# Waits for a new q tile moved to the O products, and a shorter hand-planned tail, in a gated attention and token-mixing kernel

## The chip, the cores and the metric

The kernel runs on one core of a Trainium2 chip. The time is that of the device for one execution, in microseconds (us). Work is done by TensorE (PE; its weight loads are listed apart as PEld), VectorE (DVE), ScalarE (ACT) and GpSimd (POOL); SyncE (SP) issues nearly all DMAs, in the order of its queue. Each engine works through its own queue in order and waits on semaphores.

## The reference, cut to what matters

```python
x = A_x                                        # (1, 2048, 640)
g = sigmoid((x * gate_w).sum(-1, keepdims=True))
q, k, v = x @ wq, x @ wk, x @ wv               # 32 heads of 20 for q, one shared head for k and v
a = (softmax(q k^T * 20**-0.5) v) @ wo         # per head, heads side by side: (1, 2048, 640)
h = layernorm(x)
b = (w2^T gelu(w1^T h + b1) + b2)              # mixes the 2048 tokens, inner size 1728
return g * a + (1 - g) * b
```

## The kernel before, in words

The kernel first normalizes x and projects q, k and v, and writes q to DRAM (`q_scr`). Then attention and the token-mixing products run side by side on TensorE, in one order that a planner in the program works out when it is built.

**Attention** goes by 32 units of work, n = 0 to 31: a block of 512 queries times a group of four heads. A q tile holds one such n; it is loaded from `q_scr` by six DMAs (`load_q`, L127 to L157), and its loads are issued one to several steps before its first use. Rounding of fp32 in TensorE is met by splitting numbers in a high and a low part; the products of such parts stand side by side in the contraction, 60 or 62 rows of it. For each n there are

- 64 **max tiles** (`ms_next`, L506): a product of 128 queries with 512 keys, reduced by DVE to row maxima (L514). When all 64 are through, `ms_done` and `store_max` put the negated maxima in DRAM (`m_scr`, L542) and `fetch_max` (L549) reads them back into two rows of the q tile, so that the score product subtracts them itself;
- 16 **visits** (blocks of 128 keys), each with four score products (`qk`, L688) of 62 rows, each followed by an exponential on ACT (L700), and four **O products** (`pv_mm`, L721), which stand in four column strips of TensorE and sum p times v;
- at the end, division by the row sums and a store of the split result to DRAM (`o_scr`). In the loop this is `norm_steps`, eight small steps that are taken one after the other, one in each loop step (`settle`).

Score and max products use half of TensorE's 128 rows, 0 to 63 or 64 to 127. The planner therefore keeps two **lanes**, one per half; a product of one lane can run beside one of the other.

**The other products**, also 64 rows high, fill the lanes: b1 (w1 with h), b2 (w2 with the gelu; L836), and at the end the O projection with wo (`a_jobs`, L961), which reads the stored O of one block of 128 tokens and adds the stored b part.

**The loop** (`for j in range(n_st)`) has 244 steps: 72 with b1, 128 with b2, 44 with the O projection. A step lays eight score products, some max tiles (`wants[j]`), and its share of the other products on the lanes (`arrange`), and ends with one **burst**: the 16 O products of the two visits before (`burst`), their copy out by ACT (L742) and the addition by POOL (L743). Which max tiles stand in a step follows from `wants`, and what cannot be given yet is owed. Between steps, the queues get what is due there: loads of a new q tile every eight steps, settling steps, stores, the loads for the tail (`tail_load` at steps 221 and 241 to 243), and at step 241 the last four heads' rows of wo (`last_wo`).

**Behind the loop** stand the last 24 visits, as 12 **stretches** of two visits (`stretch`): eight score products, the last 16 max tiles in the first three stretches, and the O projection of the last five token blocks as far as their heads are done, cut into jobs (`tail_job`, L910). There are nine jobs: one whole block, four blocks up to column 384, and the same four from column 384 to 560; the sums of each are taken out by DVE (L922). The order within a stretch is the best of 400 random ones by the planner's own clock (`best_order`, `trial`). Here O is summed in one bank without copies (`visits`), and the unit before the last is finished by `turned_steps`. Last come 18 products held back for the end (`held`, L1424), 128 or 48 rows high, run while DVE finishes the last unit (L812 to L817), then the products with the last four heads' wo (`final`, L1402), their way out of the accumulators (`evict`: DVE at L1411, or ACT at L1414 with POOL at L1415), and eight stores (L1437).

Waits between engines are set by hand: `touch` names for each of these instructions which others it waits for, and declares all else independent; waits on DMAs are added by the framework where a tile is used.

Of the kernel before, what the change touches and what calls it, by code (L numbers as in the profile page):

```python
# [18 lines left out]
P = 128  # L19
# [12 lines left out]
TAIL = 24  # L32
# [7 lines left out]
def mix_kernel(ctx: ExitStack, tc: tile.TileContext, A_x, A_wq, A_wk, A_wv, A_wo,  # L40
# [91 lines left out]
    def load_q(n):  # L132
# [12 lines left out]
        def part(b, j, src):  # L145
            o = 64 * b + DH * j
            rows = q_scr[src, g * 4 * DH:(g + 1) * 4 * DH, cols]
            nc.sync.dma_start(out=f32(t[o:o + DH]), in_=rows.rearrange("(a b d) q -> b d a q", a=2, b=2)[b])
# [9 lines left out]
    qtiles = {}  # L158
# [305 lines left out]
    def touch(ins, reads=(), writes=()):  # L464
        need = []
# [251 lines left out]

    def pv_mm(u, o, first, last, i):
        for hh in range(4):
# [3 lines left out]
            touch(mm, [("p", j)], [("x", i)])  # L723
# [143 lines left out]
    whole = []  # L867
    tail = [[], []]
    loaded = []
    CUT = 3 * P  # L870
# [5 lines left out]
    def room(i):  # L876
        t, at = (u0, 3 * D * i) if i < 4 else (slot[0], 3 * D * (i - 4))
        return (t[:, at:at + 2 * D].rearrange("p (j c q) -> p j c q", j=2, q=P), f32(t[:, at + 2 * D:at + 3 * D]))

    def tail_load(i):  # L880
        if i < len(jobs):
            st, r0, r1 = jobs[i]
            cols = slice(st * P, (st + 1) * P)
            oT, yt = room(i)
            c0, c1 = r0 // P, r1 // P
            for j in range(2):
                nc.sync.dma_start(out=f32(oT[:, j, c0:c1]),
                                  in_=o_scr[j, r0:c1 * P, cols].rearrange("(c p) s -> p c s", p=P))
                if r1 > c1 * P:
                    nc.sync.dma_start(out=f32(oT[:r1 - c1 * P, j, c1]), in_=o_scr[j, c1 * P:r1, cols])  # L890
            if r0 == 0:
                nc.sync.dma_start(out=yt, in_=y_scr[cols, :])
            loaded.append(i)

    def tail_job(n):
        st, r0, r1 = jobs[n]
        oT, yt = room(n)
        acc, at, ready = {}, {}, []

        def mm(c, k, d, h, first, last):  # L900
# [7 lines left out]
            r = slice(64 * h, min(r1 - c * P, 64 * h + 64))  # L908
            region = [("x", at[d, h])]
            touch(nc.tensor.matmul(acc[d, h][:, :HD2], o[r, c, :], w[r, c, d * HD2:(d + 1) * HD2],  # L910
                                   start=first, stop=last), writes=region)
            if last:
# [5 lines left out]
                if st not in parts:  # L918
                    parts[st] = fin.tile([P, D], F32, name="yo") if r1 == D else spare_row(st)
                add = parts[st] if d in ready or r0 else yt  # L920
# [3 lines left out]
                if len(ready) == 4:  # L924
                    if r1 - r0 == D:
                        whole.append(lambda: nc.sync.dma_start(out=y_out[st * P:(st + 1) * P, :], in_=parts[st]))

        for h in range(2):
            ck = [(c, k) for c in range(r0 // P, DC) if r1 - c * P > 64 * h for k in range(3)]
            for d in range(2):  # L930
                if r0 and (st, d) in held:
                    continue
                for i, (c, k) in enumerate(ck):
                    step = lambda a=(c, k, d, h, i == 0, i == len(ck) - 1): mm(*a)
                    tail[h].append((n, ("a" if i == 0 else "e" if i == len(ck) - 1 else "f", step)))
# [104 lines left out]
    aj = [a_jobs(st) for st in range(NS - 5)]  # L1040
# [23 lines left out]
    for i, j in enumerate((221, 241, 242, 243, 243)):  # L1064
        ph[j][1].append(lambda i=i: tail_load(i))
# [131 lines left out]
    for i, (st, r0, _) in enumerate(jobs):  # L1197
        tail_job(i)
# [18 lines left out]
    left, n = 64 * NU - 16 - sum(given) - sum(wants[:at]), n_st - at  # L1217
    wants[at:] = sorted(left * (i + 1) // n - left * i // n for i in range(n))
    assert sum(given) + sum(wants[:n_st - 8]) >= 64 * (NU - 1)
    owed = 0  # L1220
    for j in range(n_st):
# [6 lines left out]
        to = owed + wants[j]  # L1228
        own = round((min(to, 9) + F_US / X_US * len(fs) - len(ss)) / 2)
        if h:  # L1230
            own = (given[0] - given[1] + to + 1) // 2
        own = min(to, max(0, own))
        before = sum(given)
        ms = [[f for f in (ms_next(x) for _ in range(c)) if f] for x, c in ((h, own), (1 - h, to - own))]
        owed = to - (sum(given) - before)
# [26 lines left out]
        if j == n_st - 3:  # L1262
            raw = last_wo()
        if j == n_st - 1:
            w_last = split_last(raw)
# [3 lines left out]
    assert sum(given) == 64 * NU - 16 and not follow  # L1269
# [18 lines left out]
    def trial(kinds, prefer):  # L1288
        line, new, banks_at, held_at = list(lane), list(fresh), list(free), dict(busy)
        dve, act, now, out = clock["dve"], clock["act"], state["at"], []  # L1290
        left = [list(x) for x in kinds]
        while any(left):
            options = []
            for k in range(4):
                if left[k]:
                    at = max(line[k % 2] + W_US * new[k % 2], now)
                    if left[k][0] in "sma":
# [161 lines left out]
```

## Time and profile before

| | |
|---|---|
| median of 3 runs | 1618.53 us (1618.27 to 1618.7) |
| the profiled execution, time | 1618.5 us |
| the profiled execution, span | 1616.5 us |
| granted TensorE clock | 0.999 |
| PE, PEld, DVE, ACT, POOL busy | 1608.8, 1123.3, 1383.9, 1261.1, 841.1 us |
| loop steps with the O projection | 1331.9 to 1539.0 us from the span's start |
| stretches | 1539.0 to 1601.2 us |
| the end | 1601.2 to 1616.5 us |

Times in the profile are microseconds from the span's start unless marked ns. A row of a timeline has start, duration, engine, line, operation, out<-in by tile names, shapes and count; the bracket at its end is idle time of the engine and what ended it. "issue" there means that nothing shown was waited for. The chain of work is followed back from the last instruction, each piece to what released it. PE's matmul ends are modelled, so PE counts as busy also where the lanes are not both full.

### The profile page before, as it was taken

The numbers are of one execution on the slowest core, as the hardware profiler recorded it, in microseconds if no ns is written. First come the engines' busy times: TensorE is split into PE (matmuls) and PEld (weight loads), VectorE is DVE, ScalarE is ACT, GpSimd is POOL, SyncE is SP. The second block draws the span as 40 slices with busy tenths as digits, with TensorE's granted clock in tenths as the row PEclk, the third lists the DMA queues.
The fourth block names the chain that finished last, engine by engine and source line by source line (L and its number), as shares of the span: only waits on it lengthen the run. The fifth ranks groups of instructions, "written<-read, shape, count | busy, mean of one in ns | idle before, by whom it ended". The sixth has DMA issues, their size and how long they took to land.

```text
span 1616.5 us, 39520 instructions
## 1 busy us (share of the span) xinstructions
PE 1608.8 (100%) x14868; PEld 1123.3 (69%) x14868; DVE 1383.9 (86%) x2629; ACT 1261.1 (78%) x2350; POOL 841.1 (52%) x927
## 2 busy tenths in 40 slices
PE   9999999999999999999999999999999999999998
PEld 7899876776776776666666666666666666666665
DVE  6689899999999999888888888888888886567754
ACT  4545677777777778878888788887888879999976
POOL 6567766777787776554554334444444433333321
PEclk9999999999999999999999999999999999999999
DMA  7665322232222232222212121112221113333221
GB/s 215 206 168 144 87 66 73 61 77 69 69 70 74 53 76 63 74 68 69 69 47 64 35 61 54 58 54 60 61 60 47 54 37 112 103 115 98 85 83 59
DMA packets 180308, 129.27 MB, mean 80 GB/s; under 512 B 41585, under 2 KB 150030, under 8 KB 180118
## 3 DMA queue, kind: packets, MB, share of 16 engines
q1 hardware_dynamic: 179830, 126.43, 27.7%
q8 instruction: 117, 1.92, 0.5%
q14 instruction: 73, 0.60, 0.1%
q10 hardware_dynamic: 288, 0.33, 0.1%
HBM read 93.57 MB, written 32.15 MB: 78 GB/s over the span
## 4 chain that ended last, share of the span: by engine, by line
PE 98%; POOL 0%; DVE 0%; DMA 0%; issue 0%; ACT 0%; POOLq 0%; SPq 0%; DVEq 0%
PE xs L721 29%; PE xs L688 18%; PE xs L506 18%; PE g L836 11%; PE g L1008 7%; PE pp L302 4%; PE pu L633 4%; PE g L961 3%; PE xs L910 1%; PE x L506 1%; PE pt L294 0%; PE pp L366 0%; PE xs L1424 0%; PE pp L191 0%; PE g L688 0%
## 5 line engine op out<-in xcount | busy, mean ns | idle before, releaser
L514 DVE TENSOR_REDUCE mp<-xs 128x1 f32<-128x512 f32 x1943 | 1196.9, 684 | 154.7 <-PE xs L688 78.4
L700 ACT ACTIVATE p<-xs 128x512 f32<-128x512 f32 (+1 forms) x1834 | 1011.7, 680 | 10.9 <-PE xs L688 6.4
L743 POOL TENSOR_TENSOR osum<-osum,part 128x512 f32<-128x512 f32 x212 | 274.2, 1294 | 604.8 <-ACT part L742 597.9
L721 PE MATMUL xs<-p,v_sb 128*32 128x512 f32 x4096 | 492.3, 598 | 0.0
L688 PE MATMUL xs<-q,kst 62*128 62x512 f32 x1339 | 476.2, 417 | 1.3 <-ACT p L700 1.3
L506 PE MATMUL xs<-kst,q 60*128 60x512 f32 x1242 | 437.4, 416 | 0.0
L688 PEld LDWEIGHTS xs<-q,kst 62*128 62x128 f32 x1339 | 235.9, 185 | 74.6 <-DVE mp L514 52.3
L742 ACT ACTIVATE part<-xs 128x512 f32<-128x512 f32 x212 | 126.8, 598 | 199.6 <-PE xs L721 197.3
L1008 PE MATMUL g<-slot,w 64*128 64x320 f32 x1728 | 266.8, 306 | 0.0
L721 PEld LDWEIGHTS xs<-p,v_sb 128*32 128x32 f32 x4096 | 106.9, 109 | 225.5 <-issue 161.0
L506 PEld LDWEIGHTS xs<-kst,q 60*128 60x128 f32 x1242 | 209.6, 184 | 73.4 <-DVE mp L514 44.4
L1008 PEld LDWEIGHTS g<-slot,w 64*128 64x128 f32 x1728 | 259.1, 184 | 1.9
L127 POOL TENSOR_TENSOR w<-wr,w 128x512 fp32r<-128x512 f32 (+1 forms) x180 | 225.5, 1255 | 34.5 <-ACT w L124 22.1
L688 PE MATMUL xs<-slot,kst 62*128 62x512 f32 x567 | 206.9, 418 | 0.4 <-DVE row L922 0.2
L506 PE MATMUL xs<-kst,slot 60*128 60x512 f32 x573 | 205.3, 418 | 0.0
L836 PE MATMUL g<-u,w 64*128 64x320 f32 x1296 | 201.7, 306 | 0.0
L836 PE MATMUL g<-slot,w 64*128 64x320 f32 x1296 | 201.5, 306 | 0.0
L836 PEld LDWEIGHTS g<-u,w 64*128 64x128 f32 x1296 | 195.6, 184 | 1.7
L836 PEld LDWEIGHTS g<-slot,w 64*128 64x128 f32 x1296 | 195.6, 184 | 1.5
L688 PEld LDWEIGHTS xs<-slot,kst 62*128 62x128 f32 x567 | 99.7, 185 | 31.7 <-DVE mp L514 22.6
L506 PEld LDWEIGHTS xs<-kst,slot 60*128 60x128 f32 x573 | 96.2, 184 | 33.1 <-DVE mp L514 20.4
L961 PE MATMUL g<-slot 64*128 64x320 f32 x660 | 106.7, 306 | 0.0
(197 smaller groups left out, 1483.7 us busy)
## 6 DMA issues: line engine op xcount, KB each, us to landing
wr<-in_B_w_dram SPq DMA_DIRECT2D x155, 256.0 KB
q<-q_scr SPq DMA_DIRECT2D x126, 80.0 KB
rb<-r_scr SPq DMA_DIRECT2D x120, 64.0 KB
slot<-o_scr SPq DMA_DIRECT2D x22, 320.0 KB
y_scr<-yo SPq DMA_DIRECT2D x16, 320.0 KB
q_scr<-qh SPq DMA_DIRECT2D x19, 256.0 KB
q_scr<-ql SPq DMA_DIRECT2D x19, 256.0 KB
o_scr<-rb SPq DMA_DIRECT2D x120, 40.0 KB
```

Of the source, the lines that this page charges most:

```text
L127: nc.gpsimd.tensor_sub(wl, wr, f32(wh))
L302: nc.tensor.matmul(pp, w, t, start=first and n == 0, stop=not more and n == len(steps) - 1)
L506: mm = nc.tensor.matmul(ms, qtiles[n][64 * b:64 * b + 60, pr, qt * P:(qt + 1) * P], kst[64 * b:64 * b + 60, kq * NB:(kq + 1) * NB], start= ...
L514: red = nc.vector.tensor_reduce(out, ms, axis=AX.X, op=ALU.max)
L688: mm = nc.tensor.matmul(s, kst[64 * b:64 * b + 62, kb * P:(kb + 1) * P], q[64 * b:64 * b + 62, pr, :], start=True, stop=True)
L700: act = nc.scalar.activation(p_all[:, a * NB:(j + 1) * NB], s, AF.Exp, scale=SCALE)
L721: mm = nc.tensor.matmul(o[32 * hh:32 * hh + 32, :], v_sb[:, units[u][1], :], p_all[:, j * NB:(j + 1) * NB], start=first, stop=last, skip_g ...
L742: touch(nc.scalar.activation(part, o, AF.Copy), [("x", i)])
L743: nc.gpsimd.tensor_add(osum[n], osum[n], part)
L836: other_tile(half, nc.tensor.matmul(hold["p"][:, :HD2], w[r, fc % HS, :], u[d][r, fc, :], start=(hold["n"] == 1), stop=(hold["n"] == 6 * F ...
L961: other_tile(half, nc.tensor.matmul(hold["p"][:, :HD2], o[r, c, :], w[r, c, d * HD2:(d + 1) * HD2], start=(hold["n"] == 1), stop=(hold["n" ...
L1008: other_tile(half, nc.tensor.matmul(hold["p"][:, :HD2], w[r, st % HS, :], h[d][r, st, :], start=(hold["n"] == 1), stop=(hold["n"] == 6 * NS)))
```

## The change

It has five parts.

1. A burst's first O products each also wait for one of the six DMAs that load the q tile whose max tiles come first in the next step (`arrived`, `q_loads`; `touch` gets the list `also`). `share` is the rule that splits a step's max tiles over the lanes, taken out of the loop so that the burst can ask for the next step.
2. TAIL is 16 instead of 24: 248 loop steps and 8 stretches. A twelfth token block goes through `a_jobs` in the loop.
3. All max tiles stand in the loop, spread over the O-projection steps without the last three; the last maxima are stored one step sooner behind their split, and `fetch_max` for the last unit is called from the visit where every other unit's is.
4. The tail's jobs are four: blocks 14 and 15 up to column 384, blocks 12 and 13 up to 560, each summed in one go. So that the last 48 rows of blocks 12 and 13 can lie on different lanes, `move_wo` copies the rows of wo that they need to partitions 64 and up, and block 13's O is loaded there. `last_wo` moves to the loop's second last step, `split_last` to the first stretch; three settling steps are taken per stretch. The order search takes 300 random orders and then 3000 small mutations of the best.
5. All four pairs (block, half) of blocks 14 and 15 are held for the end, 24 products instead of 18, in the order of the column block, not of the pair: first all twelve of 48 rows, then all twelve of 128. At the end DVE empties six of the eight accumulators instead of five.

```diff
-TAIL = 24
+TAIL = 16
@@ part (load_q)
+            ins = nc.sync.dma_start(out=f32(t[o:o + DH]), in_=rows.rearrange("(a b d) q -> b d a q", a=2, b=2)[b])
+            q_loads.setdefault(n, []).append(ins)
@@ pv_mm
-            touch(mm, [("p", j)], [("x", i)])
+            touch(mm, [("p", j)], [("x", i)], [arrived.pop(0)] if arrived else [])
@@ tail
-    jobs = [(NS - 5, 0, D)]
-    jobs += [(st, 0, CUT) for st in range(NS - 4, NS)] + [(st, CUT, HEAD) for st in range(NS - 4, NS)]
-    held = ((NS - 2, 0), (NS - 2, 1), (NS - 1, 0))
+    jobs = [(st, CUT) for st in (NS - 2, NS - 1)] + [(st, HEAD) for st in (NS - 4, NS - 3)]
+    held = tuple((st, d) for st in (NS - 2, NS - 1) for d in range(2))
...
+    def move_wo():
+        for i, w in enumerate((wo_hi, wo_lo)):
+            t = slot[0][:, i * D:(i + 1) * D]
+            nc.sync.dma_start(out=f32(t[64:64 + HEAD - (DC - 1) * P]), in_=f32(w[:HEAD - (DC - 1) * P, DC - 1, :]))
+            low_wo.append(t)
@@ loads of the tail
-    for i, j in enumerate((221, 241, 242, 243, 243)):
-        ph[j][1].append(lambda i=i: tail_load(i))
+    for j, (st, _) in zip((241, 242, 243, 244), jobs):
+        ph[j][1].append(lambda st=st: tail_load(st, 0, CUT))
+    ph[n_st - 8][1].append(move_wo)
@@ burst
+        if len(wants) > us[1] // 2 + 2:
+            counts = share(us[1] // 2 + 2)
+            n = max((given[b] + counts[b] - 1) // 32 for b in range(2))
+            if n in qtiles:
+                arrived.extend(q_loads.pop(n, ()))
@@ fetch_at
-        if kb == 11 and n + 2 < NU:
+        if kb == 11 and n + 1 < NU:
@@ max tiles
-    left, n = 64 * NU - 16 - sum(given) - sum(wants[:at]), n_st - at
-    wants[at:] = sorted(left * (i + 1) // n - left * i // n for i in range(n))
+    left, n = 64 * NU - sum(given) - sum(wants[:at]), n_st - 3 - at
+    wants[at:] = sorted(left * (i + 1) // n - left * i // n for i in range(n)) + [0] * 3
@@ loop, between steps
+            if len(row_max) == NU and follow:
+                follow.pop(0)()
+                stores.pop()()
...
-        if j == n_st - 3:
+        if j == n_st - 2:
             raw = last_wo()
@@ best_order
-        for _ in range(400):
+        for _ in range(300):
...
+        for n in range(3000):
+            order = list(best[1])
+            for _ in range(rng.choice((1, 1, 2, 3))):
+                order.insert(rng.randrange(len(order)), order.pop(rng.randrange(len(order))))
+            score = trial(kinds, order)
+            if score[0] <= best[0]:
+                best = score
@@ stretch
-            ms = [("m", ms_next(b)) for _ in range((3, 3, 2)[i] if i < 3 else 0)]
...
-        settle()
-        settle()
-        pop_chain()
-        if i in (7, 8):
-            tail_load(2 * i - 9)
-            tail_load(2 * i - 8)
+        if i == 0:
+            w_last.extend(split_last(raw))
+        for _ in range(3):
+            settle()
+        if i in (2, 3):
+            for st in range(NS + 2 * i - 8, NS + 2 * i - 6):
+                tail_load(st, CUT, HEAD)
@@ held products
-    for st, d in held:
-        oT, _ = room(jobs.index((st, CUT, HEAD)))
-        for c in range(DC - 1, CUT // P - 1, -1):
-            r = min(P, HEAD - c * P)
+    for c in range(DC - 1, CUT // P - 1, -1):
+        r = min(P, HEAD - c * P)
+        for st, d in held:
+            oT, _ = room(st)
@@ end
-                evict(i, d, (i, d) in ((1, 0), (1, 1), (2, 1), (3, 1)))
+                evict(i, d, (i, d) not in ((0, 1), (2, 0)))
```

More of the change, by code (lines that the diff above doesn't have):

```diff
@@ L918, in mm @@
                 if st not in parts:
[L919 to L920 removed]
+                    parts[st] = spare_row(st)
+                add = parts[st] if d in ready else yt
                 ready.append(d)
@@ L1195, in burst @@
         fresh[:] = [True, True]
-    for i, (st, r0, _) in enumerate(jobs):
+    for i in range(len(jobs)):
         tail_job(i)
@@ L1227, in mix_kernel @@
         fs, rest, done = ph[j]
[L1228 to L1235, printed above, removed]
+        counts, before = share(j), sum(given)
+        ms = [[f for f in (ms_next(x) for _ in range(counts[x])) if f] for x in (h, 1 - h)]
+        owed = sum(counts) - (sum(given) - before)
         pop_chain()
@@ L1376, in next_acc @@
         return i
-    assert not tail[0] and not tail[1] and not any(later) and not whole
+    assert not tail[0] and not tail[1] and not any(later)
     pool = pools["last"]
```

124 lines of the change are left out of this document (57 added, 67 removed).

## The prediction

> **What bounds the kernel now.** I read the shares of the page's chain first, then a table of windows cut at the starts of O-product bursts, then the end of the timeline.
>
> ```profile
> PE 98%; POOL 0%; DVE 0%; DMA 0%; issue 0%; ACT 0%; POOLq 0%; SPq 0%; DVEq 0%
> ```
>
> TensorE carries 98% of the chain, so the change is worth what it takes off TensorE's own queue. The windows below are, in order: the 26 loop steps with four max tiles, the 18 with five, the first four stretches behind the loop, the other eight, and the end. The first columns are length, PE, PEld, DVE, ACT and POOL busy; PE is busy all the time up to the last eight.
>
> ```profile
> 1331.90:1452.08 120.18, 120.18 (x1120) 75.00 (x1119) 74.29 (x152) 116.80 (x234) 40.69 (x39) 1.00 0.36 109
> 1452.08:1538.98 86.90, 86.90 (x794) 54.20 (x793) 60.70 (x121) 81.49 (x163) 27.51 (x27) 1.00 0.33 98
> 1538.98:1561.59 22.61, 22.61 (x197) 14.44 (x197) 14.56 (x29) 17.06 (x35) 6.66 (x8) 1.00 0.27 85
> 1561.59:1601.15 39.56, 39.19 (x359) 24.50 (x358) 15.07 (x30) 32.28 (x66) 1.90 (x2) 1.00 0.16 44
> 1601.15:1616.50 15.35, 10.98 (x75) 7.11 (x74) 6.61 (x16) 4.01 (x9) 2.61 (x3) 0.93 0.24 86
> ```
>
> So an O-projection step costs 120.18/26 = 4.62 us with four max tiles and 86.90/18 = 4.83 us with five; the first four stretches average 5.65 us, the last eight 4.945 us. ScalarE is busy 116.80/26 = 4.49 us of each four-tile step (nine instructions: eight exponentials, one copy of the O sum) but only 32.28/8 = 4.04 us of a late stretch, which has no copy. From 1331.90 to 1601.15 there are 56 such pieces in 269.25 us; after the change there are 56 as well, 48 steps and 8 stretches.
>
> **Part 1: O products take over the waits for a new q tile.** In the b2 stage a step runs from one burst to the next. A plain step and one with the first max products of a new tile:
>
> ```profile
> 1247.44 1.92 PE L721 MATMUL xs<-p,v_sb 128*32 128x512 f32 x16
> 1253.01 1.92 PE L721 MATMUL xs<-p,v_sb 128*32 128x512 f32 x16
> 1258.69 0.64 PE L721 MATMUL xs<-p,v_sb 128*32 128x512 f32 x4
> ...
> 1297.90 1.92 PE L721 MATMUL xs<-p,v_sb 128*32 128x512 f32 x16
> 1303.59 0.64 PE L721 MATMUL xs<-p,v_sb 128*32 128x512 f32 x4
> L506 PEldq EVENT_SEMAPHORE  x64: 51/51/51, 626.1 to 1303.1; - x64
> ...
> 1603.75 0.13 PEld L721 LDWEIGHTS xs<-p,v_sb 128*32 128x32 f32 x4 [0.30 <-issue]
> ```
>
> Plain: 5.57 us. New tile: 5.68 and, at the end of the stage, 5.69 us. The row of L506 counts the separate wait instructions ahead of max products in this stage: 64, four for each of 16 tiles, 51 ns each and always already satisfied. They stand between row-tiled products, where the queue has no slack: 0.11 us a tile, 16 x 0.11 = 1.8 us. In the earlier b1 stage a step has more max tiles and the excess is unclear; I count nothing. In the O-projection stage ScalarE is busy 97% and I also count nothing.
>
> What it adds: six waits on the first six O products of one burst per tile. The burst's weight loads run ahead of the products and then idle 0.30 us in every group of four (last row, from a late burst), and all but the first carry no wait now. The first already waits for ScalarE, so it may need one separate 51 ns wait, which can run while the last max products finish. I take 0; the ends are 0 and 0.11 us a tile (the whole price again), and more only where a load is late, which is rival (c). Whoever is behind these products on TensorE waits with them, so the loads must have landed:
>
> ```profile
> 1241.54 2.19 SPq L148 DMA_DIRECT2D q<-q_scr  x6
> ```
>
> This tile's first max products are in the step that begins at 1253.01 us; its six loads are all issued by 1243.73 us, so the burst comes 9.3 us later. Part 1: -1.8 us (0 to -2.1, the latter with three tiles of b1).
>
> **Part 2: four more steps, eight stretches, no max tiles behind the loop.** Before, 194 max tiles fall on 44 steps (26 with 4, 18 with 5) and 16 on three stretches. After, 210 fall on 45 steps: 15 with 4, 30 with 5; the last three steps have none. Those three exist nowhere now. From below, ScalarE still does its nine instructions, 4.49 us; from above, a four-tile step, 4.62 us. I take 4.50, since four max products fewer leave TensorE shorter than that; if ScalarE overlaps better, 4.3 is possible.
>
> For the stretches, two rows of the chain, with the bursts that begin and end one of them:
>
> ```profile
> 1581.81 1.85 PE xs L721 x16
> ...
> 1586.62 1.85 PE xs L721 x16
> ```
>
> The eight stretches have 180 row-tiled projection products (90 a lane) where the last eight had some 165 (88 and 77): lanes even at last, the longer one 2 products longer. A fifth max tile, 512 columns wide, adds 0.21 us to a step; a projection product has 320 columns, 0.13 us by its width: +0.3 us by the longer lane, and +1.0 us if the 15 products in all share two lanes without any slack. Each of the four jobs now sums all its columns in one go, so DVE empties 16 accumulators in 8 stretches instead of 30 in 12. The order search also tries 3000 mutations instead of only 400 random orders. The best stretch now took 1586.62 - 1581.81 = 4.81 us against 4.945 on average, so some 0.13 a stretch is there; I take 0.05, -0.4 in all.
>
> The last max rows must reach the q tile before the first stretch.
>
> ```profile
> 1528.54 0.62 POOL L982 MEMSET yo<- 128x640 f32 x1
> 1549.35 1.30 POOL L770 TENSOR_TENSOR osum<-osum,rb 128x512 f32<-128x512 f32 x1 [6.35 <-DMA rb<-r_scr]
> ...
> 1531.73 1.48 SPq L985 DMA_DIRECT2D yo<-in_A_wo_dram  x4
> 1545.16 2.55 SPq L767 DMA_DIRECT2D rb<-r_scr  x4
> 1560.87 2.75 SPq L549 DMA_DIRECT2D slot<-m_scr  x4
> ...
> 1561.60 1.95 DMA slot<-m_scr
> ...
> 1566.92 1.90 PE xs L721 x16
> ...
> PE xs L688 <- DMA slot<-m_scr: 0.2, 1, 0.2
> ```
>
> Now this path costs 0.2 us of waiting. After, count from the burst of step 245 (zero). The store of the maxima waits for DVE's work behind that step's products, 0.5 by estimate; then SP's four rb loads behind it, landed 4.2 us later as here (1545.16 to 1549.35) at about 5; POOL's scaling 1.3 and the memset of the last wo rows 0.6, to 7; SP's four wo loads 1.5, to 8.5; only then the four m loads, 0.69 us apart, landing 1.95 us after issue at 10.4, 11.1, 11.8 and 12.5. The first stretch begins two steps and a burst later, 4.5 + 4.5 + 1.9 = 10.9. The lane that needs the last two loads may stop for up to 1.6 us, depending on where its first score product stands; I take 0.6. The present 0.2 us goes, with the stretch in which it stands (1561.59 to 1566.92, 5.3 us against 4.945 on average): -0.4.
>
> The other loads I count as covered. Those of columns 384 to 560 follow the turned O tile of unit 30; a third settling per stretch brings that chain forward by about a stretch, and they are needed from the end of the fourth stretch on. If they are late, that stretch and the next wait, which the bound below takes in.
>
> Sum: 15 x 4.62 + 30 x 4.83 + 3 x 4.50 = 227.7; stretches 39.56 + 0.3 - 0.4 + 0.6 - 0.4 = 39.7; together 267.4 against 269.25: -1.9 us. Ends: steps at 4.3 (-0.6), every stretch at 4.81 (38.5 instead of 39.1 without the stall, -0.6) and no stall (-0.6) give -3.7; steps at 4.62 (+0.4), products by their sum (+0.7), a 1.6 us stall (+1.0) and no better order (+0.4) give +0.7. The two copies of wo rows and one more row block's loads are issued on SP some steps ahead of the chain of the m rows, which waits for other engines at its start; were SP full there, each would push it by 0.37 us (1.48/4).
>
> **Part 3: the end.** Weight loads, products, and what follows them:
>
> ```profile
> 1604.72 0.44 PEld L1424 LDWEIGHTS xs<-slot,slot 48*128 48x128 f32 x3 [0.84 <-issue]
> 1605.35 0.45 PEld L1424 LDWEIGHTS xs<-slot,slot 128*128 128x128 f32 x3 [0.19 <-issue]
> ...
> 1604.72 3.89 PE L1424 MATMUL xs<-slot,slot 48*128 48x320 f32 x18
> 1607.13 0.42 DVE L817 TENSOR_TENSOR q<-part,q 128x256 fp32r<-128x256 f32 x1
> 1608.45 1.04 PE L1402 MATMUL xs<-row,q 128*128 128x320 f32 x6
> 1611.45 1.74 POOL L1415 TENSOR_TENSOR p<-p,row 128x320 f32<-128x320 f32 x2 [0.38 <-ACT p L1414]
> 1612.17 0.55 DVE L1411 SCALAR_TENSOR_TENSOR p<-xs,g_col,row 128x320 f32<-128x320 f32 x1 [0.33 <-PE xs L1402]
> 1613.22 0.90 ACTq L1437 DMA_DIRECT2D out_dram<-p  x2
> ```
>
> The held products end when the final ones begin, and what these need from DVE is there at 1607.55, so held products are on the path. The 18 come in six groups of three, alternately 48 and 128 rows. The second group starts 0.63 us after the first, of which the three loads take 0.44 and the idle time at the change of height 0.19. After: 24 products as twelve of 48 rows, then twelve of 128: 24 x 0.15 + 2 x 0.19 = 3.98 us against 3.89: +0.1 us, where 24 at the present mean would be +1.3. The Trainium skill ("TensorEngine Tiling (Array Packing)", Key Properties) says that changing the tiling mode drains TensorE while changing tiles within a mode does not; that agrees with the idle 0.19 us ahead of each group here.
>
> Then the last two stores wait on ScalarE's queue for POOL's add of row block 3, left half, done at 1613.19, while DVE is done with the right half at 1612.72. DVE takes that half over: its last operation starts at 1612.17; with one more of 0.55 us just ahead of it, it ends about 0.2 us later, so the last store is issued about 0.6 us earlier. Part 3: -0.5 us (-0.8 to +0.8).
>
> Sum: -1.8 - 1.9 - 0.5 = -4.2 us. The profiled execution took 1618.5 us (span 1616.5), the median of the runs is 1618.53, so both give 1614.3 us.
>
> **The rivals.** (a) The waits only move, or the separate wait instructions stay: part 1 is nothing, 1616.1 us. For it: the first O product has its wait slot taken. Against: 0.30 us of slack in each group of loads.
> (b) The stretches give the gain back: fuller lanes (+1.0 instead of +0.3), a 1.6 us stall and no better order make part 2 +0.3, 1616.5 us. For it: the SP order above. With (a) as well 1618.3.
> (c) Slower: a burst now stands until the last of six loads has landed. Place: the burst ahead of a tile's first use, 28 tiles; it decides from (4.2 + 3.2)/28 = 0.26 us a tile; 0.5 us of stop would give 1614.3 + 14 = 1628 us. Against: 9.3 us between issue and burst here, and loads land within 2 to 4.2 us in the rows above. The rule that speaks for it: the Trainium skill ("DMA: Bandwidth & Descriptors", Rules for kernel authors) advises to wait on a DMA's semaphore late, and this change waits earlier; no row here shows a q load landing that late.
>
> **How the numbers follow.** A measurement of this kernel tells about 0.2%, 3.2 us, from no change, so faster means under 1615.3. The forecast, 1612 to 1615.3 on its own, gets 0.64; (a) 0.12 and (b) 0.14 fall within 0.2%; (c) and other late data on SP's queue 0.10. Faster 0.64, same 0.26, slower 0.10. The range from 1611.8 (the better ends of all three parts, -2.1 - 3.7 - 0.8) to 1617.0 (past (a) or (b) alone, short of both) leaves 2 in 10 out.
>
> **What would show it.** Right: new-tile steps of the b2 stage at 5.57 us and the 64 separate waits gone; 30 steps of 4.83, three near 4.5; stretches near 4.95 with the first one longer; held products in about 4.0 us with two height changes; last store on ScalarE's queue before POOL matters. Wrong: bursts longer than 1.92 us with a DMA as releaser, a wait of score products for m rows over 1.6 us, or stretches over 5.1 us.

## The result

The changed kernel took 1613.24 us (median of 7 runs, 1612.93 to 1613.6), the kernel before beside it 1618.35 us (7 runs, 1618.06 to 1618.94): a ratio of 0.9967, 95% interval 0.9959 to 0.9976. That is 5.1 us faster (3.9 to 6.6 by the interval), against 4.2 forecast. The profiled execution took 1613.6 us, its span 1611.7 us against 1616.5.

In the page of the changed kernel, the busy times and the shares of the chain of waits:

```profile
PE 1603.9 (100%) x14865; PEld 1118.7 (69%) x14865; DVE 1378.1 (86%) x2622; ACT 1262.4 (78%) x2353; POOL 844.7 (52%) x930
...
PE 99%; ACT 1%; POOL 0%; DVE 0%; issue 0%; DVEq 0%; POOLq 0%
```

TensorE is still the chain; the gain is 4.9 us of its busy time (1608.8 before). The stages are cut at the same places as in the prediction, at starts of O-product bursts. First the b2 stage, from the burst of step 71 to that of step 198, of the kernel before and then of the changed one; columns are length, then PE, PEld, DVE, ACT and POOL busy, granted clock, DMA share and GB/s.

```profile
618.69:1331.90 713.21, 713.21 (x6638) 480.04 (x6636) 637.68 (x1191) 581.23 (x1049) 325.59 (x353) 1.00 0.20 58
```
```profile
618.83:1329.92 711.09, 711.09 (x6638) 477.07 (x6637) 637.76 (x1193) 581.31 (x1049) 325.35 (x353) 1.00 0.20 58
```

Then the rest of the changed kernel: 15 steps with four max tiles, 30 with five, the three without any, the first stretch, the second, the other six, and the end:

```profile
1329.92:1399.31 69.39, 69.39 (x646) 43.24 (x646) 43.54 (x89) 67.11 (x135) 21.41 (x21) 1.00 0.37 110
1399.31:1544.23 144.92, 144.92 (x1322) 90.33 (x1321) 101.43 (x203) 135.66 (x271) 46.73 (x44) 1.00 0.36 106
1544.23:1556.96 12.73, 12.73 (x118) 7.84 (x117) 1.73 (x8) 12.43 (x27) 6.19 (x8) 1.00 0.21 56
1556.96:1562.78 5.82, 5.51 (x49) 3.53 (x48) 1.65 (x4) 5.55 (x12) 4.53 (x6) 1.00 0.35 112
1562.78:1567.84 5.06, 5.06 (x49) 3.20 (x48) 2.83 (x6) 4.44 (x10) 1.00 (x1) 1.00 0.12 28
1567.84:1596.10 28.26, 28.26 (x277) 17.72 (x276) 6.77 (x13) 23.71 (x48) 1.90 (x2) 1.00 0.15 38
1596.10:1611.70 15.60, 11.07 (x82) 7.98 (x80) 7.51 (x18) 3.76 (x8) 1.74 (x2) 0.99 0.24 86
```

| | before, us | after, us | difference | forecast |
|---|---|---|---|---|
| b2 stage | 713.21 | 711.09 | -2.12 | -1.8 |
| ahead of it | 618.69 | 618.83 | +0.14 | 0 |
| 48 steps and 8 stretches (before: 44 and 12) | 269.25 | 266.18 | -3.07 | -1.9 |
| the end, from the last burst | 15.33 | 15.63 | +0.30 | -0.5 |

The sum is -4.75 us; the spans differ by 4.8. (The ends of the last row are unrounded; the window rows cut at the span's rounded end.) Two terms were larger than forecast, and the end came out with the wrong sign.

The waits in the b2 stage: two plain bursts and one ahead of a new tile's first max products, and the separate wait instructions at the O products in that stage.

```profile
1245.66 1.92 PE L724 MATMUL xs<-p,v_sb 128*32 128x512 f32 x16
1251.24 1.92 PE L724 MATMUL xs<-p,v_sb 128*32 128x512 f32 x16
1256.80 0.64 PE L724 MATMUL xs<-p,v_sb 128*32 128x512 f32 x4
```
```profile
L724 PEldq EVENT_SEMAPHORE  x16: 51/51/51, 623.9 to 1295.5; - x16
```

The 64 separate waits at the max products are gone. One per tile has come up at the O products, 51 ns, but the step with the new tile (1251.24 to 1256.80) takes 5.56 us, like the plain one (5.58).

The first stretch waits for max rows. SP's and POOL's queues ahead of it, and the separate waits on TensorE's queue ahead of the score products of the first stretch (1557 to 1563 us):

```profile
1549.81 1.77 SPq L770 DMA_DIRECT2D rb<-r_scr  x4
1555.30 1.41 SPq L989 DMA_DIRECT2D yo<-in_A_wo_dram  x4
1556.76 2.80 SPq L550 DMA_DIRECT2D slot<-m_scr  x4
```
```profile
1553.42 1.28 POOL L773 TENSOR_TENSOR osum<-osum,rb 128x512 f32<-128x512 f32 x1 [0.77 <-DMA rb<-r_scr]
1554.64 0.63 POOL L986 MEMSET yo<- 128x640 f32 x1
```
```profile
L689 PEldq EVENT_SEMAPHORE  x2: 51/51/51, 1559.6 to 1560.9; - x2
```

This is the queue that the prediction laid out: rb loads, POOL's scaling and memset, the wo loads, and only then the four m loads. Counted from the burst of step 245 (1548.47 us), they have landed 10.4, 11.1, 11.7 and 12.4 us later; the prediction had 10.4, 11.1, 11.8 and 12.5. The two waits end 0.08 us behind the landing of the second and of the fourth load (1559.55 and 1560.87 us), and the score products with these rows start at once behind them. The profile's list of waits puts this pause down to ScalarE (`PE xs L689 <- ACT p L701`); the landings show that it is the m rows.

The held products' weight loads, which show the heights (first figure of "48*128" is the rows):

```profile
1599.67 0.45 PEld L1436 LDWEIGHTS xs<-slot,u 48*128 48x128 f32 x3 [0.84 <-issue]
...
1601.62 0.45 PEld L1436 LDWEIGHTS xs<-slot,u 128*128 128x128 f32 x3 [0.19 <-issue]
...
1603.35 0.77 PEld L1414 LDWEIGHTS xs<-row,q 128*128 128x128 f32 x5
```

24 products with one change of height inside. From the first load (1599.67) to the first load of the final products behind them it is about 3.7 us, against 3.6 (1604.72 to 1608.31) for 18 before.

### The profile page after: what moved, and what is told of

It reads as the page before. It is cut to its first block, busy times and chain, and to the rows that moved or that the text cites. A ratio compares the mean times of both kernels' runs of the same rounds, so it can differ in the third digit from the quotient of the medians.

```text
span 1611.7 us, 39437 instructions
## 1 busy us (share of the span) xinstructions
PE 1603.9 (100%) x14865; PEld 1118.7 (69%) x14865; DVE 1378.1 (86%) x2622; ACT 1262.4 (78%) x2353; POOL 844.7 (52%) x930
## 4 chain that ended last, share of the span: by engine, by line
PE 99%; ACT 1%; POOL 0%; DVE 0%; issue 0%; DVEq 0%; POOLq 0%
PE xs L724 30%; PE xs L689 18%; PE xs L507 18%; PE g L839 11%; PE g L1012 7%; PE pp L303 4%; PE pu L634 4%; PE g L965 3%; PE x L507 1%; PE xs L919 1%; PE pp L367 0%; ACT p L701 0%; PE pt L295 0%; PE xs L1436 0%; PE pp L192 0%; PE g L919 0%
## 5 line engine op out<-in xcount | busy, mean ns | idle before, releaser
L701 ACT ACTIVATE p<-xs 128x512 f32<-128x512 f32 (+1 forms) x1840 | 1013.9, 678 | 4.0 <-PE xs L689 2.9
L746 POOL TENSOR_TENSOR osum<-osum,part 128x512 f32<-128x512 f32 x216 | 279.2, 1293 | 615.5 <-ACT part L745 599.1
L689 PE MATMUL xs<-q,kst 62*128 62x512 f32 x1344 | 477.0, 418 | 1.3 <-ACT p L701 1.3
L507 PE MATMUL xs<-kst,q 60*128 60x512 f32 x1242 | 432.8, 415 | 0.0
L689 PEld LDWEIGHTS xs<-q,kst 62*128 62x128 f32 x1344 | 236.6, 185 | 74.8 <-DVE mp L515 53.9
L689 PE MATMUL xs<-slot,kst 62*128 62x512 f32 x568 | 206.2, 417 | 0.3 <-ACT p L701 0.3
L689 PEld LDWEIGHTS xs<-slot,kst 62*128 62x128 f32 x568 | 99.6, 185 | 30.5 <-DVE mp L515 21.8
L965 PE MATMUL g<-slot 64*128 64x320 f32 x720 | 118.2, 306 | 0.0
```

The costliest lines, as they stand in the source:

```text
L507: mm = nc.tensor.matmul(ms, qtiles[n][64 * b:64 * b + 60, pr, qt * P:(qt + 1) * P], kst[64 * b:64 * b + 60, kq * NB:(kq + 1) * NB], start= ...
L689: mm = nc.tensor.matmul(s, kst[64 * b:64 * b + 62, kb * P:(kb + 1) * P], q[64 * b:64 * b + 62, pr, :], start=True, stop=True)
L701: act = nc.scalar.activation(p_all[:, a * NB:(j + 1) * NB], s, AF.Exp, scale=SCALE)
L746: nc.gpsimd.tensor_add(osum[n], osum[n], part)
L965: other_tile(half, nc.tensor.matmul(hold["p"][:, :HD2], o[r, c, :], w[r, c, d * HD2:(d + 1) * HD2], start=(hold["n"] == 1), stop=(hold["n" ...
```

## The experiments

### Part 1 alone, and the change without it

e1_before_waits is the kernel before with the waits at the O products and nothing else of the change (`share`, `q_loads` and the argument `also` of `touch` come with it):

```diff
+        if len(wants) > us[1] // 2 + 2:
+            counts = share(us[1] // 2 + 2)
+            n = max((given[b] + counts[b] - 1) // 32 for b in range(2))
+            if n in qtiles:
+                arrived.extend(q_loads.pop(n, ()))
```

> The kernel before with part 1 alone (O products take over the waits for a new q tile). My account: the two traces differ by 2.1 us between the bursts of the b2 stage, so this kernel takes 2.0 to 2.3 us off 1618.4, about 1616.2, its 16 new-tile steps at 5.58 us. Rival: the gain of those steps comes with the new wants or the tail, then it stays within 0.5 us of 1618.4.

Measured: 1616.2 us against 1618.78 beside it, ratio 0.9984 (0.9975 to 0.9993). Its b2 stage:

```profile
619.11:1330.32 711.21, 711.21 (x6639) 477.07 (x6637) 637.48 (x1191) 581.24 (x1049) 325.38 (x353) 1.00 0.20 58
```

e2_after_no_waits is the changed kernel with that part taken out:

```diff
-                arrived.extend(q_loads.pop(n, ()))
+                q_loads.pop(n, ())
```

> The changed kernel without part 1: O products wait for no DMA, the max products wait as before. My account: 2.0 to 2.3 us above the changed kernel, about 1615.4, the separate waits ahead of max products back, new-tile steps at 5.69 us, the tail unchanged. Rival: the tail also lives on the earlier waits, then it is over 3 us above.

Measured: 1615.89 us, ratio 0.9981 (0.9972 to 0.999). Its b2 stage, and its separate waits at the max products:

```profile
618.66:1331.85 713.19, 713.19 (x6638) 479.92 (x6637) 637.46 (x1191) 581.24 (x1049) 325.49 (x353) 1.00 0.20 57
```
```profile
L507 PEldq EVENT_SEMAPHORE  x115: 51/51/51, 97.1 to 1422.3; - x115
```

In the changed kernel 11 of these are left. Both ways round the stage moves by 2.0 to 2.1 us and part 1 is worth what it was said to remove; rival (a) is out. The medians say 2.6 us for it both ways (1618.78 - 1616.2, 1615.89 - 1613.24), 0.5 more than this stage shows. Ten more tiles have their separate waits outside this stage ((115 - 11 - 64)/4), but the stage ahead of it takes 618.5 to 619.7 us from profile to profile, with part 1 and without, so where the 0.5 us lies is not shown; the spread of single runs is as large.

### What the stretches owe to the search, to the m rows and to the sums

e3_random_orders undoes the search: 400 random orders, no mutations.

```diff
-        for _ in range(300):
+        for _ in range(400):
...
-        for n in range(3000):
+        for n in range(0):
```

> The changed kernel whose stretches take the best of 400 random orders, as before, without the 3000 mutations. The late stretches average 4.71 us where I forecast about 4.85. Account A: the search does it, then the last six stretches lose 0.1 to 0.2 us each, 0.6 to 1.3 us in all. Rival B: the four longer sums with 16 instead of 30 emptied accumulators do it, then the time stays within 0.3 us of the changed kernel.

Measured: 1613.92 us, ratio 0.9969 (0.9956 to 0.9981), span 1612.0. The eight stretches took 39.06 us against 39.14 in the changed kernel. The last six took 28.43 us against 28.26. Over all eight the search gives nothing, in the last six at most 0.2 us: the account that put 0.6 to 1.3 us on it falls, and with it the prediction's reason for -0.4 us. The median is 0.7 us above the changed kernel's, but the kernel before, measured beside it, was 0.4 us slower too (1618.78 against 1618.35).

e4_wo_later moves the loads of the last wo rows one step back, behind the m loads:

```diff
-        if j == n_st - 2:
+        if j == n_st - 1:
             raw = last_wo()
```

> The changed kernel with the load of the last wo rows one loop step later, so that SP issues the four loads of the m rows ahead of it. The first stretch takes 5.82 us. My account: it waits for these m rows, which are issued 8.3 us behind the burst of step 245 because POOL's scaling, its memset and the wo loads stand ahead; then the m loads go out some 5 us sooner, the first stretch takes 4.7 to 5.0 us and the time falls by 0.8 to 1.1 us, to about 1612.3. Rival, as the list of waits has it: the exponentials hold the score products there, then nothing changes, within 0.2 us.

Measured: 1612.67 us, ratio 0.9961 (0.9949 to 0.9974), span 1611.0: the fastest kernel here together with e11, 0.6 us below the changed one by medians. SP's queue, and the windows of the first stretch, the second and the other six:

```profile
1551.54 2.79 SPq L550 DMA_DIRECT2D slot<-m_scr  x4
1559.51 0.67 SPq L989 DMA_DIRECT2D yo<-in_A_wo_dram  x2
```
```profile
1556.83:1561.99 5.16, 5.16 (x49) 3.32 (x49) 1.65 (x4) 5.16 (x12) 3.86 (x5) 1.00 0.15 42
1561.99:1567.06 5.07, 5.07 (x51) 3.17 (x49) 2.83 (x6) 4.58 (x10) 2.30 (x2) 1.00 0.41 131
1567.06:1595.34 28.28, 28.28 (x277) 17.74 (x276) 6.74 (x13) 23.69 (x48) 1.91 (x2) 1.00 0.15 38
```

The m loads are issued at 1551.54 instead of 1556.76 us, the first stretch falls from 5.82 to 5.16 us and PE is busy all through it; the other seven stay. So the first stretch's excess was the wait for the m rows, 0.66 us, and it came from the order on SP. That is one pair of profiles: in the ten profiles with the old order on SP the first stretch takes 5.66 to 6.01 us, in e4 and e11 5.16, so 0.5 to 0.85 us.

e5_split_sums cuts the sums of blocks 12 and 13 in two again, at column 384, so that DVE empties 24 accumulators behind the loop instead of 16:

```diff
+                cuts = [i for i, (c, k) in enumerate(ck) if c * P == CUT and k == 0]
                 for i, (c, k) in enumerate(ck):
-                    step = lambda a=(c, k, d, h, i == 0, i == len(ck) - 1): mm(*a)
+                    a0, e0 = i == 0 or i in cuts, i == len(ck) - 1 or i + 1 in cuts
+                    step = lambda a=(c, k, d, h, a0, e0): mm(*a)
```

> The changed kernel, but blocks 12 and 13 are summed in two goes again, cut at column 384, so that 24 instead of 16 accumulators are emptied in the stretches; the products and the lanes stay. The order search has been shown not to be the cause of the late stretches' 4.71 us. Account B: the longer sums are (fewer accumulators to wait for and to empty), then the last six stretches lose some 0.1 us each, 0.4 to 1.0 us in all. Rival C: the even lanes are, then it stays within 0.2 us of the changed kernel.

Measured: 1613.76 us, ratio 0.9969 (0.9956 to 0.9981), span 1612.0. The last six stretches, and the end:

```profile
1567.81:1596.88 29.07, 28.99 (x278) 17.77 (x277) 11.26 (x21) 24.02 (x48) 1.90 (x2) 1.00 0.15 38
1596.88:1612.00 15.12, 11.06 (x81) 7.98 (x80) 7.39 (x18) 3.55 (x8) 1.74 (x2) 1.00 0.24 88
```

29.07 us against 28.26, with DVE at 11.26 us instead of 6.77: summing in one go makes the late stretches shorter, by 0.8 us in six. Six at the kernel before's mean of 4.945 us would be 29.67, 1.4 us more than here; what holds the other 0.6 us no run shows, beyond the 0.2 us of e3. Little of that shows in the time, because the end is 0.5 us shorter here for another reason, below.

### The end

e6_evict_before gives DVE back only the share of the accumulators that it had before (row block 3, left half, goes by ScalarE and POOL again):

```diff
-                evict(i, d, (i, d) not in ((0, 1), (2, 0)))
+                evict(i, d, (i, d) in ((1, 0), (1, 1), (2, 1), (3, 1)))
```

> The changed kernel with the accumulator of block 13's sister, row block 3 left half, emptied by ScalarE and POOL as before, not by DVE. The changed kernel's last store is issued 12.02 us behind the last burst (before 12.54) but lands at 14.75 (before 14.43). Account A: issuing sooner only crowds the stores, and an instruction load in their midst costs the last one 0.5 us; then this kernel's end is 15.2 to 15.5 us, the time 0.1 to 0.4 us below the changed kernel. Rival B, as forecast: the last store's issue sets the end, then the end is 16.2 to 16.3 us, the time 0.6 us above.

Measured: 1614.6 us, ratio 0.9975 (0.9964 to 0.9985); the profiled execution 1613.9. POOL's last adds and the last two stores:

```profile
1606.11 1.74 POOL L1427 TENSOR_TENSOR p<-p,row 128x320 f32<-128x320 f32 x2 [0.38 <-ACT p L1426]
...
1607.88 1.88 ACTq L1449 DMA_DIRECT2D out_dram<-p  x2
```

Against the changed kernel's

```profile
1607.37 1.09 ACTq L1449 DMA_DIRECT2D out_dram<-p  x2
```

The first store of the pair is issued as soon as POOL's add is done, 12.16 us behind the last burst's start instead of 11.27. But the pair also takes 1.88 us instead of 1.09, and that is not POOL: the first issue itself lasts 1.40 us instead of 0.38. ScalarE's issues in the changed kernel and then in e6 (ns min/median/max):

```profile
L1449 ACTq DMA_DIRECT2D out_dram<-p x2: 338/358/379, 1607.4 to 1608.1; - x2
```
```profile
L1449 ACTq DMA_DIRECT2D out_dram<-p x2: 384/890/1397, 1607.9 to 1609.4; - x2
```

The long issue begins 12.16 us behind the burst, and from 12.05 to 12.41 us the DMA engines load 8 KB of instructions; whether that is its cause no run shows. The end grows from 15.63 to 16.39 us. With an issue of 0.38 us it would be some 15.4 us by estimate (16.39 - 1.02), 0.3 above the 15.1 us of the runs further down whose last store lands in one piece. So the takeover by DVE is worth something, since all eight runs of e6 (1613.7 us and up) lie above all runs of the changed kernel (up to 1613.6); how much stays open between 0.3 us and the 1.4 us of the medians (0.9 with each taken against the kernel before beside it). The rival, that the crowding of stores alone sets the end, forecast a time 0.1 to 0.4 us below the changed kernel's; the times say otherwise, but its end of 15.2 to 15.5 us is what the estimate gives.

e7_held_by_pair runs the 24 held products pair by pair, as the kernel before did with its 18:

```diff
-    for c in range(DC - 1, CUT // P - 1, -1):
-        r = min(P, HEAD - c * P)
-        for st, d in held:
-            oT, _ = room(st)
+    for st, d in held:
+        oT, _ = room(st)
+        for c in range(DC - 1, CUT // P - 1, -1):
+            r = min(P, HEAD - c * P)
```

> The changed kernel with its 24 held products ordered by accumulator as before: eight groups of three, alternately 48 and 128 rows. My account: each change of height costs 0.19 us, eight instead of two, 6 x 0.19 = 1.15 us more, held products 5.0 us instead of 3.8, the time 1.0 to 1.2 us above the changed kernel. Rival: DVE's last unit work is the bound at that place, then at most 0.2 us.

Measured: 1614.58 us, ratio 0.9973 (0.9963 to 0.9983). The weight loads:

```profile
1599.12 0.45 PEld L1436 LDWEIGHTS xs<-slot,u 48*128 48x128 f32 x3 [0.84 <-issue]
1599.75 0.44 PEld L1436 LDWEIGHTS xs<-slot,u 128*128 128x128 f32 x3 [0.19 <-issue]
1600.38 0.44 PEld L1436 LDWEIGHTS g<-slot,u 48*128 48x128 f32 x3 [0.19 <-issue]
...
1603.56 0.45 PEld L1436 LDWEIGHTS xs<-slot,u 128*128 128x128 f32 x3 [0.19 <-issue]
```

0.19 us ahead of each group, seven times instead of once, and the end is 16.79 us against 15.63: +1.17 us for six changes of height (6 x 0.19 = 1.14). The Trainium skill ("TensorEngine Tiling (Array Packing)", Key Properties) has the rule that changing the mode drains TensorE; by that rule, the trace agrees, and the price here is 0.19 us a change.

### What an earlier wait costs when the loads are late

e8_late_loads issues the loads of each later q tile two loop steps later, with part 1 in place:

```diff
-        if j % 8 == 7:
-            u = j // 8
+        if j in (7, 15) or j % 8 == 1 and j > 17:
+            u = (j - 2) // 8 if j > 15 else j // 8
```

> The changed kernel with each q tile from the eighth on loaded two loop steps later, shortly ahead of the burst that now waits for it. This measures rival (c) of the forecast. Account: the loads start at the burst and their six issues take 2.2 us, landing some 2 us later; the first O products stand for 1 to 3 us per tile, 16 tiles of the b2 stage, 15 to 50 us in all. Rival: SP runs far enough ahead of TensorE that the loads are still issued early, then it stays within 1 us of the changed kernel.

e9_late_no_waits is the same without part 1:

> The late loads of the run before, but without part 1: only the max products wait for them. In the run with part 1 four of 16 tiles stopped a step, by 0.27 to 0.88 us, 2.3 us together. Account: waiting at the burst costs this because the wait stands up to one step ahead of the need; here these four steps keep 5.7 us or less and only the 0.11 us of separate waits return at each tile, 1.8 us in all, so the b2 stage is 0 to 0.7 us shorter than with part 1. Rival: the max products meet the same late loads, then the four steps are long again and the stage is 1 to 2 us longer than with part 1.

Measured: 1615.64 and 1616.26 us, one run each. The b2 stages of e8 and e9, and, between them, the loads that e8's O products waited for in that stage (us, times):

```profile
618.57:1332.11 713.54, 713.54 (x6638) 478.16 (x6637) 637.55 (x1193) 581.23 (x1049) 325.39 (x353) 1.00 0.20 57
```
```profile
  DMA slot<-q_scr: 3.3, 11
  DMA q<-q_scr: 0.8, 3
```
```profile
619.70:1332.72 713.02, 713.02 (x6638) 479.98 (x6637) 637.77 (x1191) 581.30 (x1049) 325.85 (x353) 1.00 0.21 57
```

With the late loads the b2 stage of e8 is 2.45 us longer than in the changed kernel; four of its 16 new-tile steps take 5.84 to 6.46 us. Without part 1 the same late loads stop nothing (1.93 us, the price of the separate waits). So rival (c) exists and costs 2.45 us in this stage, 0.5 us more than part 1 saves, but at two steps' delay it is far smaller than was expected: at 12 of the 16 tiles the loads were still there in time. The whole times go the other way, e9 being 0.6 us slower, but its stage ahead of b2 took 1.1 us longer (619.70 us against 618.57), so only the stage is compared here. The Trainium skill ("DMA: Bandwidth & Descriptors", Rules for kernel authors) advises to wait late; here that held only where the loads had been issued later (2.45 us against 1.93).

### More and fewer max tiles to a step

e10_even_counts gives the 45 steps four or six max tiles, never five, so that the lanes are even:

```diff
-    wants[at:] = sorted(left * (i + 1) // n - left * i // n for i in range(n)) + [0] * 3
+    pairs_of = left // 2
+    wants[at:] = sorted(2 * (pairs_of * (i + 1) // n - pairs_of * i // n) for i in range(n)) + [0] * 3
```

> The changed kernel with even numbers of max tiles in the O-projection steps: 30 steps of 4 and 15 of 6 instead of 15 of 4 and 30 of 5. From the traces, none gives 4.24, four 4.62, five 4.83 us: the first four cost 0.095 each, the fifth 0.21. Account: an odd count leaves the lanes uneven, so six take about as long as five, 4.85 to 4.95; then 30 x 4.62 + 15 x 4.9 = 212.1 against 214.2, 1 to 2.5 us less. Rival: each further tile costs 0.21, six take 5.04, then 214.2, no change.

Measured: 1613.52 us, ratio 0.9967 (0.9954 to 0.9979). Fifteen of its steps with four, its fifteen with six, and its three without:

```profile
1399.14:1468.49 69.35, 69.35 (x646) 43.25 (x645) 42.12 (x87) 67.76 (x137) 23.17 (x22) 1.00 0.31 94
1468.49:1544.50 76.01, 76.01 (x675) 47.72 (x674) 58.68 (x116) 67.91 (x136) 23.67 (x22) 1.00 0.39 116
1544.50:1557.24 12.74, 12.74 (x120) 7.85 (x119) 2.40 (x9) 12.43 (x27) 6.24 (x8) 1.00 0.18 54
```

4.62, 5.07 and 4.25 us a step. A sixth max tile costs 0.24 us, a little more than the fifth, so even counts win nothing.

e11_even_wo_later has both edits of e10 and e4.

> Even counts together with the later load of the last wo rows. If even counts are worth 1 to 2.5 us and the later load 1.0 us, and neither touches the other, the time is 2.0 to 3.5 us under the changed kernel; if only the latter counts, 1.0 us.

Measured: 1612.63 us, ratio 0.9963 (0.995 to 0.9975), span 1610.9; stretches 38.50 us as in e4. No better than e4 (1612.67), and 0.6 us below e12, the changed kernel on the same chip (1613.22). But its end is 15.09 us, 0.5 below the changed kernel's, with the same code there. The DMA queues in the last stores' time, 1608.5 to 1611 us in the changed kernel and then 1608 to 1610.9 us in e11 (packets, MB, share of the 16 DMA engines):

```profile
q10 hardware_dynamic: 271, 0.31, 34.8%
q1 hardware_dynamic: 150, 0.17, 18.2%
q14 instruction: 1, 0.01, 0.8%
```
```profile
q10 hardware_dynamic: 288, 0.33, 31.3%
q1 hardware_dynamic: 207, 0.22, 21.4%
```

And SP's closing waits for the stores (ns min/median/max), of the changed kernel and of e11; the longest is 0.53 us longer in the changed one:

```profile
L1467 SPq EVENT_SEMAPHORE  x7: 17/28/1435, 1608.0 to 1611.7; - x7
```
```profile
L1469 SPq EVENT_SEMAPHORE  x7: 17/28/901, 1607.7 to 1610.8; - x7
```

In the changed kernel a load of instructions (one packet of 8 KB) falls among the last store's packets: 15 of that store's 16 parts have landed 14.19 us behind the last burst's start, the sixteenth at 14.75. The same holds in e2, e3, e4, e8 and e9, with the load there: landed at 14.74 to 14.76, end 15.63 to 15.65; in e7, with a later end, the sixteenth part is 0.56 us late as well. In all of these the load starts 1.44 to 1.49 us behind the issue of that store. In e5, e10 and e11 no such load is there, the last store has landed at 14.20 or 14.21, and the end is 15.08 to 15.09 us; in e6 the load came before the last store's issue, and no part is late. That the load makes the difference is a comparison of profiles: these kernels differ in other places too, and no run moved the load alone.

### The changed kernel again

> The changed kernel itself, as the base for the other runs of this group: 5.1 us under the kernel before, the end again some 15.6 us with an instruction load among the last stores.

e12_changed_again is the changed kernel unedited, on the chip of e9 to e11: 1613.22 us, ratio 0.9966 (0.9952 to 0.9979), 5.6 us under the kernel before beside it (1618.82). First stretch 5.66 us against 5.82, end 15.66 us against 15.63; the instruction load is again among the last packets, and the last store landed at 14.77 us. So the first stretch moves by 0.16 us between two executions of one kernel, and the end by 0.03.

## Why the prediction was right, and where it was not

**Bound.** TensorE stayed on the chain for 99% of it; that the change is worth what it takes off TensorE's queue held throughout.

**Part 1, forecast -1.8 us, measured -2.12.** Right in place and mechanism (e1, e2). The size was low by 0.02 us a tile: 2.12/16 = 0.13 us instead of 0.11, which was read off one pair of steps. The added separate wait, taken as 0 between 0 and 0.11, is there (16 of 51 ns) and is hidden, as argued from the 0.30 us of slack in each group of the burst's loads: the new tile's step is no longer than the plain one.

**Part 2, forecast -1.9 us, measured -3.07.** Step by step:

- Steps with four and five max tiles: 69.39/15 = 4.63 and 144.92/30 = 4.83, as forecast.
- Steps without max tiles: forecast 4.50, measured 12.73/3 = 4.24. This is the step that failed in size, -0.8 us of the gap. I took ScalarE's busy time in a four-tile step, 4.49 us, as a floor, and left 4.3 as possible if ScalarE overlaps better. The floor isn't one. The exponentials of those three steps, and how ScalarE runs them:

```profile
L701 ACT ACTIVATE p<-xs x25: 592/679/852, 1543.4 to 1556.8; 128x512 f32<-128x512 f32 x25
```
```profile
1546.28 0.60 ACT L745 ACTIVATE part<-xs 128x512 f32<-128x512 f32 x1 [0.30 <-PE xs L724]
1546.77 2.55 ACT L701 ACTIVATE p<-xs 128x512 f32<-128x512 f32 x5
```

  Five exponentials of a median 0.68 us fill only 2.55 us: neighbours overlap. Over the whole execution consecutive exponentials start 0.477 us apart in the median and never under 0.472. Nine such starts are 4.25 to 4.29 us, and the three steps take 4.24. A four-tile step takes 4.62 us for the same nine starts, with pauses between some of them; there the busy time also counts the end of each instruction that no neighbour covers (0.63 us long in the median), so a busy share of 97% said little of how much shorter the step could be. The Trainium skill ("ScalarE: Activation LUTs", What ACT_TABLE_LOAD costs) says that activations one behind another overlap by about 93 ns; by that rule the trace agrees in kind, with 0.12 us for the shortest (0.59 - 0.47) and 0.2 us for the median (0.68 - 0.48). That ScalarE is what limits these steps is argued from these starts, of which 23 of 25 are within 0.485 us; TensorE is busy in them too, and no run tested it.
- Stretches: 39.14 us against 39.7 forecast. The m rows' wait was forecast 0.6 and came out as 0.66 (e4; 0.5 to 0.85 over the profiles), by the queue on SP that the prediction counted out. The later stretches, 28.26/6 = 4.71 us, beat what was forecast, in good part because each job is summed in one go, with fewer accumulators to empty (e5: +0.8 us when undone); the better search, to which the prediction gave its -0.4 us, did nothing over the eight (e3). So the stretches came near their forecast partly by luck: the -0.4 us, which the sum calls a better order, came from elsewhere, mainly from the sums, which the prediction named but did not price.

**Part 3, forecast -0.5 us, measured +0.30.** The sign was wrong. Held products cost about +0.1 us, as forecast; the takeover moved the last store's issue from 12.54 to 12.02 us behind the last burst's start, 0.52 of the 0.6 us forecast; what that is worth by itself e6 leaves open. What failed is the step from the issue of the last store to the end, taken as unchanged: the store landed at 14.75 us instead of 14.43. From issue to landing it took 2.73 us instead of 1.89. Of the 0.84 us, 0.56 is its last part, which is late in every profile with the instruction load among its packets. The other 0.3 goes with closer stores (all eight are now issued within 3.4 us, before in 4.0): in e10 and e11 the last is issued another 0.28 us earlier, at 11.74, and lands no earlier than the first fifteen parts do here, 14.20; that these 0.3 us come from the crowding is argued, not tested. In the runs without the load the end is 15.1 us, -0.25 against before, half of the forecast.

**Rivals.** (a) fell with e1 and e2. (b) needed slow stretches; of its three mishaps the wait was there and the search gave nothing, but the longer sums outweighed both; what the fuller lanes cost no run shows. (c) did not occur: the plain step is as long as the new tile's, and e8 and e9 show what it takes.

The forecast of 1614.3 us came within 1.1 us because errors of both signs partly cancelled: part 1 gave 0.3 and part 2 1.2 us more, part 3 0.8 us less, and the stage ahead, put at nothing, took 0.1 longer. The rest, between the spans' -4.8 and the medians' -5.1, lies between runs. In the forecast's range the lower end is 0.1 us off its own sum (1618.5 - 6.6 is 1611.9), on which nothing hangs.

## What to carry to other kernels

A wait that is always satisfied still costs on a full queue, and the same wait is free on an instruction that has slack: find the 51 ns instructions and the nearest idle gap ahead of them. Don't take an engine's busy time as the floor of a step when its instructions overlap; count starts (here nine of 0.477 us), in a stretch where it runs without gaps. When a shorter tail lets a chain start earlier, write out the one DMA queue it passes through; here the order of two groups of loads on SP was worth 0.5 to 0.85 us of a stretch.

## What was not expected of the hardware

- Max tiles have no single price beside the other work of a step: with none 4.24 us, four 4.62 (0.095 each), the fifth 0.21, the sixth 0.24.
- The last part of a store, with one 8 KB instruction load among its packets, landed 0.55 to 0.57 us behind the other fifteen, in both profiles of the changed kernel and in the six others with such a load there; where it was not, no part came late.
- One issue of a store on ScalarE's queue lasted 1.40 us instead of 0.38 (e6); such a load ran as it began.
- Waiting for a q tile's loads up to a step early cost nothing with loads issued as they were, and 2.45 us over 16 tiles with loads two steps later, 0.5 more than the separate waits that it replaces (1.93).
